# A decode kernel that streams its weights: contiguous MLP weights, a block transpose on VectorE, and a head's output weights on three DMA engines

## The chip, the cores and the metric

The kernel runs on one core of a Trainium2 chip. The metric is the device time of one execution in microseconds; the time before is the median of seven runs. A profile of one execution goes with it. All of the work is memory traffic with small computations on it: four sequences, one new token each.

## What is computed

Cut to what matters (B = 4, D = 512, 32 query heads on 8 key/value heads of 128, F = 1792, bfloat16):

```python
xn = layernorm(x)
# attention over the last W = 1024 cached positions, 4 query heads per cache head
q = xn @ wq;  p = softmax(q k^T * 128 ** -0.5);  s = (p v) @ wo
# MLP
h = gelu(layernorm(xn) @ w1 + b1)
g = silu(h @ w2 + b2)
return x + s * g
```

## The kernel before

All loads of weights and caches are issued by SyncE (SP) onto one queue, in the order in which they are used: wq's first half, K of heads 0 and 1, wq's second half, K of heads 2 to 7, V of head 0, w1, V of head 1, w2, V of heads 2 to 7, and last wo in six transfers. One queue is spread over sixteen DMA engines; each transfer raises a semaphore by 16 when all of it is there. `kv_buf` has eight slots, so V of a head is loaded into the slot of the K that has been transposed (L205 waits for `t_last`). wo's loads (L475) wait for nothing. The small loads of x, b1, b2 and of x in 16 rows (`x16`, L251, in two parts of eight rows) are issued by ScalarE (ACT).

A little planner (`_Program`) keeps one list of operations per engine, in the order in which the code adds them, and puts semaphore waits ahead of an operation. The order on TensorE (PE) is thus that of the code: transposes of K in groups of eight (`T`, L278) run eight groups ahead of the scores (`S`, L297). Then, per head, `PV` (L315) with a product that sums the probabilities (L321); VectorE (DVE) follows with the epilogue (L328 to L333) that divides. Around head 0 to 2 stand the MLP's parts.

The first MLP layer (`mlp1`, L395) has the four tokens, padded to 32 columns, as the stationary operand, and w1 as the moving one. The 14 chunks of 128 hidden values are covered by four column groups of the PE array, `K0 = (0, 4, 8, 10)`, each of 512 columns, with an overlap. Its moving operand is taken in steps: hidden value `p * 14 + k` belongs to chunk k, so that a chunk can be contracted with w2's rows as they lie in memory. GELU runs over 128 by 512 values (L410 to L419). `mlp2` turns the result with four PE transposes (L424) and a copy (L429); `mlp3` multiplies by w2 (L442); `mlp4` makes the gate `g_sb`.

At the end the heads' outputs `OTb` (hidden index on partitions) have to stand as wo's rows do: with `wo_r`, partition p of a head holds the four rows 4p to 4p+3, a contiguous 4 KB. `to_rows` (L486) does that with 16 matmuls by the selector `sel`, and a cast to `OW` (L493). `wo` (L507) then multiplies, transfer by transfer as they land: heads 0 and 1, 2 and 3, 4 and 5, head 6, three of head 7's four rows, and its last row. Each transfer's matmuls have wo as the stationary operand (128 by 128) and four columns moving. L534 multiplies by the gate, L538 turns 16 columns into 16 rows, L540 adds x16, L542 stores.

Of the kernel before, what the change touches and what calls it, by code (L numbers as in the profile page):

```python
# [16 lines left out]
class _Program:  # L17
# [10 lines left out]
    def add(self, eng, fn, *deps):  # L28
        op = _Op(eng, fn, deps)
        self.ops[eng].append(op)  # L30
        return op
# [42 lines left out]
def bass_recurrent_scan__sliding_block_cached__mixer_channel_mlp__decode_kernel(  # L74
# [14 lines left out]
    ALU = mybir.AluOpType  # L89
    AF = mybir.ActivationFunctionType  # L90
    AX = mybir.AxisListType
    BF16 = dt.bfloat16
    F32 = dt.float32

    B, D = 4, 512
    HQ, HKV, DH = 32, 8, 128
# [3 lines left out]
    F = B_w1.shape[1]  # L100
    FC = F // 128
    NC = 32
    KR = W // NC
    UT = 8
# [17 lines left out]
    wo_sb = sb([128, HKV, 4, D], BF16)  # L122
    w1_sb = sb([128, 4, F], BF16)
    w2_sb = sb([128, FC, D], BF16)
    kt_buf = sb([128, NKT, UT * 128], BF16)
    P_buf = sb([128, HKV, NC * 16], BF16)

# [31 lines left out]
    b2_sb = sb([4, 128], BF16)  # L159
    sel = sb([128, 4, 32], BF16)  # L160
    OW = sb([128, 4, HKV * 4], BF16)
    hT = sb([128, 64], BF16)

    OTb = sb([128, HKV * 16], BF16)
    den_sb = sb([128, HKV * 16], F32)
# [38 lines left out]
    def load_v(g):  # L204
        d_v[g] = pg.dma("sp", "v%d" % g, lambda e: e.dma_start(  # L205
            kv_buf[:, (HKV + g) % NS, :, :].rearrange("p c d -> p (c d)"), cache_rows(A_v_cache, g)),
            t_last[(HKV + g) % NS] if HKV + g >= NS else None)
# [11 lines left out]
    for g in range(2, HKV):  # L219
# [11 lines left out]
    c_sel = add("gp", lambda e: e.affine_select(  # L231
        sel[:, :, :], ones_bf[:, :], [[1, 4], [4, 32]], ALU.is_equal, 0.0,
        base=0, channel_multiplier=-1), c_1)
    c_xT = add("gp", lambda e: e.memset(xT[:, :, :], 0.0))
    c_yT = add("gp", lambda e: e.memset(yT[:, :, :], 0.0))
    c_z = add("gp", lambda e: e.memset(zero_bf[:, :], 0.0))
# [4 lines left out]
    c_id32 = add("gp", lambda e: e.affine_select(  # L241
        ident32[:, :], ones32[:, :], [[1, 128]], ALU.is_equal, 0.0,
        base=0, channel_multiplier=-1), c_o32)


    v = add("dve", lambda e: e.tensor_copy(x32[:, :], x_bf[:, :]), d_x)  # L246
# [1 line left out]
    v = add("dve", lambda e: e.bn_aggr(mv1[:, :], st1[:, :]), v)  # L248
    v = add("dve", lambda e: e.tensor_single_scalar(vt1[:, :], mv1[:, 1:2], EPS, ALU.add), v)
    a = add("act", lambda e: e.activation(sq1[:, :], vt1[:, :], AF.Sqrt), v)  # L250
    d_x16 = [pg.dma("act", "x16%d" % i, lambda e, i=i: e.dma_start(  # L251
        x16[8 * i:8 * i + 8, :], x_r[8 * i:8 * i + 8, :])) for i in range(2)]
    v = add("dve", lambda e: e.reciprocal(rstd1[:, :], sq1[:, :]), a)
    v = add("dve", lambda e: e.tensor_scalar(xn32[:, :], x32[:, :], mv1[:, 0:1], rstd1[:, 0:1],
                                             op0=ALU.subtract, op1=ALU.mult), v)
# [10 lines left out]
    cp = {}  # L266
# [116 lines left out]

    K0 = (0, 4, 8, FC - 4)
    mlp = {}

    def f32k(n):

        return kt_buf[:, n, :].bitcast(F32)
    hb = kt_buf[:, 4, 0:512]
    h_ps = psK[0][:, 0:1024].bitcast(F32)

    def mlp1():  # L395
        def fn(pe):
            last = None
            for c in range(4):
                for s in range(4):
                    pe.matmul(psK[0][32 * s:32 * s + 32, 0:1024].bitcast(F32), yT[:, c, :],  # L400
                              bass.AP(w1_sb, c * F + K0[s], [[4 * F, 128], [1, 4], [FC, 128]]),
                              start=(c == 0), stop=False, tile_position=(0, 32 * s))
            for s in range(4):
                last = pe.matmul(psK[0][32 * s:32 * s + 32, 0:1024].bitcast(F32),
                                 ones_bf[0:1, 0:32],
                                 bass.AP(b1_sb, K0[s], [[F, 1], [1, 4], [FC, 128]]),
                                 start=False, stop=True, tile_position=(0, 32 * s))
            return last
        t = add("pe", fn, v_xyT, d_w1, d_b1, *[cp[n] for n in range(NUN - NB, NUN)])
        a = add("act", lambda e: e.activation(f32k(0), h_ps, AF.Square), t)  # L410
        v = add("dve", lambda e: e.scalar_tensor_tensor(f32k(1), f32k(0), 1.0 / GELU_K, h_ps,  # L411
                                                        op0=ALU.add, op1=ALU.mult), a)
        mlp["t"] = add("act", lambda e: e.activation(f32k(2), f32k(1), AF.Tanh,
                                                     scale=GELU_C * GELU_K), v)

    def mlp2():
        v = add("dve", lambda e: e.tensor_scalar(f32k(3), f32k(2), 0.5, 0.5,
                                                 op0=ALU.mult, op1=ALU.add), mlp["t"])
        v = add("dve", lambda e: e.tensor_tensor(hb, f32k(3), h_ps, ALU.mult), v)  # L419

        def fn(pe):
            last = None
            for t in range(4):
                last = pe.transpose(psK[2][:, t * 128:(t + 1) * 128],  # L424
                                    kt_buf[:, 4, t * 128:(t + 1) * 128], ident[:, :])
            return last
        t = add("pe", fn, v, cp[NUN - 1], cp[NUN - 2])

        mlp["h"] = add("dve", lambda e: e.tensor_copy(  # L429
            bass.AP(hT, 0, [[64, 128], [4, 16], [1, 4]]),  # L430
            bass.AP(psK[2], 0, [[1024, 128], [32, 16], [1, 4]])), t)

    def mlp3():
        def fn(pe):
            last = pe.matmul(psM[:, PS_Z:PS_Z + 16], b2_sb[:, :],
                             bass.AP(ident, 0, [[128, 4], [1, 4], [0, 4]]),
                             start=True, stop=False, skip_group_check=True)
            for k in range(FC):
                s = min(k // 4, 2) if k < FC - 4 else 3
                n = (k - K0[s]) * 16 + s * 4  # L440
                for c in range(4):
                    last = pe.matmul(psM[:, PS_Z + c * 4:PS_Z + (c + 1) * 4],  # L442
                                     w2_sb[:, k, c * 128:(c + 1) * 128], hT[:, n:n + 4],
                                     start=False, stop=(k == FC - 1), skip_group_check=True)
            return last
        t = add("pe", fn, mlp["h"], d_w2, d_b2, c_id)
        mlp["tz"] = add("act", lambda e: e.activation(
            tz_sb[:, :], psM[:, PS_Z:PS_Z + 16], AF.Tanh, scale=0.5), t)
# [8 lines left out]
    for n in range(LAG, NUN + LAG):  # L457
# [6 lines left out]
    load_v(1)  # L464
    d_w2 = pg.dma("sp", "w2", lambda e: e.dma_start(
        w2_sb[:, :, :], B_w2.rearrange("(p c) o -> p c o", c=FC)))
    for g in range(2, HKV):
        load_v(g)

    wo_r = A_wo.rearrange("(g p i) o -> p g i o", g=HKV, i=4)  # L470
    d_wo = []
    for n, (g0, g1, i0, i1) in enumerate(((0, 2, 0, 4), (2, 4, 0, 4), (4, 6, 0, 4), (6, 7, 0, 4),
                                          (7, 8, 0, 3), (7, 8, 3, 4))):
        d_wo.append((g0, g1, i0, i1, pg.dma("sp", "wo%d" % n, lambda e, g0=g0, g1=g1, i0=i0, i1=i1:
                                            e.dma_start(wo_sb[:, g0:g1, i0:i1, :],  # L475
                                                        wo_r[:, g0:g1, i0:i1, :]))))

    def to_rows(g0, g1):

        psx = psS[0]  # L480

        def fn(pe):
            last = None
            for i in range(4):
                for j in range(4):
                    last = pe.matmul(psx[32 * j:32 * j + 32, i * 32 + g0 * 4:i * 32 + g1 * 4],  # L486
                                     sel[:, i, :],
                                     bass.AP(OTb, g0 * 16 + j * 4,
                                             [[HKV * 16, 128], [16, g1 - g0], [1, 4]]),
                                     start=True, stop=True)  # L490
            return last
        t = add("pe", fn, ep[g1 - 1], c_sel, ex[HKV - 2])
        return add("dve", lambda e: e.tensor_copy(  # L493
            OW[:, :, g0 * 4:g1 * 4],
            psx[:, 0:128].rearrange("p (i n) -> p i n", i=4)[:, :, g0 * 4:g1 * 4]), t)

    first = [True]

    def wo(k, rows):
        g0, g1, i0, i1, d = d_wo[k]  # L500

        def fn(pe):
            last = None
            for g in range(g0, g1):
                for i in range(i0, i1):
                    for c in range(4):
                        last = pe.matmul(psM[:, PS_W + c * 4:PS_W + (c + 1) * 4],  # L507
                                         wo_sb[:, g, i, c * 128:(c + 1) * 128],
                                         OW[:, i, g * 4:(g + 1) * 4],
                                         start=first[0], stop=(k == len(d_wo) - 1 and i == i1 - 1),  # L510
                                         skip_group_check=True)
                        first[0] = False
            return last
        return add("pe", fn, d, rows, mlp["g"])

    for g in range(HKV):
        PV(g)
        if g == 0:
            epilogue(0)
            mlp1()  # L520
        if g >= 2:
            epilogue(g - 1)
        if g == 1:
            mlp2()
            mlp3()
        if g == 2:
            mlp4()
    epilogue(HKV - 1)
    rows = to_rows(0, HKV)
    for k in range(len(d_wo)):  # L530
        t_w = wo(k, rows)


    v = add("dve", lambda e: e.tensor_tensor(  # L534
# [61 lines left out]
```

## Time and profile before

| | |
|---|---|
| median of 7 runs | 77.05 us (76.97 to 77.1) |
| profiled execution | 77.07 us |
| its span, first to last instruction | 75.3 us |
| mean granted TensorE clock | 0.829 |
| busy: PE, weight loads, DVE, ACT, POOL | 51.3, 39.5, 39.2, 9.8, 4.6 us |
| moved by DMA | 28.99 MB in 4219 packets |
| code fetched on queue q8 | 8 packets, 0.13 MB |
| first MLP layer, L400: 16 matmuls | 4.9 us busy, 1085 ns each |
| query projection, L362: 32 matmuls | 1.9 us busy, 380 ns each |
| output product, L507: 128 matmuls | 3.9 us busy, 166 ns each |

The granted clock of TensorE is at 0.9 or more of full speed in the first 28 of 40 slices of the span and at about half in the last ones. Matmuls overlap, so a group's busy time is shorter than the number of matmuls times the mean of one. A row of the time line gives start, length (both in us), engine, line, operation, target and source, count, and in brackets how long the engine was idle before and what released it. SPq and ACTq are the queues' issuing instructions. In the chain of work that ended last, "issue" is time for which the profile shows no reason.

### The profile page before, as it was taken

The page shows a single profiled execution, that of the slowest core. Times are in us where ns is not written, and L with a number is a line of the kernel's source. Part 1 is how long each engine was busy: PE and PEld are TensorE (multiplying, and loading weights), DVE is VectorE, ACT ScalarE, POOL GpSimd, SP SyncE. Part 2 cuts the span into 40 slices and gives each one's busy share as a digit, 9 for nine tenths or more (in the row PEclk, how much of TensorE's full clock was granted, in tenths as well). Part 3 has the DMA queues.
Part 4 walks back from the last instruction along what each step waited for, and adds up shares of the span by engine and source line. Part 5 has one row for each costly group of instructions (what it writes and reads, how often), then busy time and mean ns, then how long its engine had stood idle before and what let it go on. Part 6 is the DMA issues. An engine that isn't in the chain of part 4 may idle for free.

```text
span 75.3 us, 2309 instructions
## 1 busy us (share of the span) xinstructions
PE 51.3 (68%) x1058; PEld 39.5 (52%) x1058; DVE 39.2 (52%) x82; ACT 9.8 (13%) x16; POOL 4.6 (6%) x14
## 2 busy tenths in 40 slices
PE   0000039984779939987996995999069999918760
PEld 0000039973269929977995880104059586518740
DVE  0778106795158957985995505001664679770010
ACT  0611000000180303111130440003300000000000
POOL 6980000000000000000000000000000000000000
PEclk9999999999999999999999997589555555555555
DMA  2899999998999999999999999999999999999700
GB/s 45 244 418 416 429 440 462 453 418 379 418 440 431 418 422 418 435 414 467 411 408 445 418 428 409 427 422 409 418 435 431 425 401 420 420 418 407 269 19 2
DMA packets 4219, 28.99 MB, mean 385 GB/s; under 512 B 493, under 2 KB 625, under 8 KB 1650
## 3 DMA queue, kind: packets, MB, share of 16 engines
q1 hardware_dynamic: 4160, 28.84, 92.2%
q8 instruction: 8, 0.13, 0.6%
q10 hardware_dynamic: 50, 0.01, 0.1%
q14 instruction: 1, 0.01, 0.0%
HBM read 28.85 MB, written 0.00 MB: 383 GB/s over the span
## 4 chain that ended last, share of the span: by engine, by line
DMA 37%; PE 34%; SPq 16%; issue 5%; DVE 5%
DMA wo_sb<-in_A_wo_dram 24%; PE psK L278 21%; SPq L475 15%; DMA kv_buf<-in_A_k_cache_dram 12%; PE psS L297 6%; DVE kt_buf L284 3%; PE psO L362 3%; PE psS L293 2%; DVE q_sb L368 1%; PE psM L507 1%; PE psK L374 1%; PE psK L346 1%; PE psS L538 1%; SPq L212 1%; SPq L205 0%
## 5 line engine op out<-in xcount | busy, mean ns | idle before, releaser
L278 PE MATMUL psK<-ident,kv_buf 128*128 128x128 bf16 x256 | 20.8, 234 | 12.2 <-DMA kv_buf<-in_A_k_cache_dram 10.7
L284 DVE COPY kt_buf<-psK 128x1024 bf16<-128x1024 bf16 x32 | 21.2, 691 | 9.0 <-PE psK L278 8.9
L278 PEld LDWEIGHTS psK<-ident,kv_buf 128*128 128x128 bf16 x256 | 16.8, 106 | 11.5 <-DMA kv_buf<-in_A_k_cache_dram 10.7
L297 PE MATMUL psS<-qT,kt_buf 128*128 128x16 bf16 x256 | 10.4, 169 | 1.3 <-issue 1.3
L297 PEld LDWEIGHTS psS<-qT,kt_buf 128*128 128x128 bf16 x256 | 9.4, 96 | 3.2 <-issue 2.3
L315 PEld LDWEIGHTS psO<-P_buf,kv_buf 128*128 128x128 bf16 x256 | 7.4, 102 | 3.0 <-issue 3.0
L315 PE MATMUL psO<-P_buf,kv_buf 128*128 128x16 bf16 x256 | 8.0, 173 | 0.2
L328 DVE TENSOR_REDUCE den_sb<-psS 128x16 f32<-128x512 f32 x8 | 5.5, 691 | 4.2 <-PE psS L321 4.0
L305 ACT ACTIVATE P_buf<-psS 128x512 bf16<-128x512 f32 x8 | 4.8, 597 | 17.6 <-PE psS L297 17.6
L400 PE MATMUL psK<-w_sb,yT 128*32 128x512 bf16 x16 | 4.9, 1085 | 0.8 <-issue 0.8
L507 PE MATMUL psM<-OW,wo_sb 128*128 128x4 bf16 x128 | 3.9, 166 | 1.2 <-issue 0.6
L507 PEld LDWEIGHTS psM<-OW,wo_sb 128*128 128x128 bf16 x128 | 3.7, 104 | 1.4 <-issue 1.2
L321 PE MATMUL psS<-P_buf,ones_bf 128*128 128x512 bf16 x8 | 4.3, 534 | 0.0
L411 DVE SCALAR_TENSOR_TENSOR kt_buf<-kt_buf,psK 128x512 f32<-128x512 f32 x1 | 0.7, 686 | 6.1 <-ACT kt_buf L410 6.1
L293 PE MATMUL psS<-negm,ind 128*128 128x512 bf16 x8 | 3.0, 380 | 0.0
L534 DVE TENSOR_TENSOR sg_sb<-psM,g_sb 128x16 f32<-128x16 f32 x1 | 0.2, 185 | 4.7 <-PE psM L507 4.7
L400 PEld LDWEIGHTS psK<-w_sb,yT 128*32 128x32 bf16 x16 | 0.5, 114 | 3.6 <-issue 3.6
L369 ACT ACTIVATE q_sb<-psO 128x512 bf16<-128x512 f32 x1 | 0.6, 597 | 13.3 <-PE psO L362 13.3
L331 DVE RECIPROCAL rden<-den_sb 128x16 f32<-128x16 f32 x8 | 2.0, 253 | 0.3
L362 PE MATMUL psO<-wq_sb,xT 128*32 128x512 bf16 x32 | 1.9, 380 | 0.3 <-DVE xT L351 0.3
L424 PE MATMUL psK<-ident,kt_buf 128*128 128x128 bf16 x4 | 0.6, 308 | 2.1 <-DVE kt_buf L419 2.1
L246 DVE CAST P_buf<-x_bf 4x512 f32<-4x512 bf16 x1 | 0.8, 816 | 2.4 <-DMA x_bf<-in_A_x_dram 2.4
(64 smaller groups left out, 28.8 us busy)
## 6 DMA issues: line engine op xcount, KB each, us to landing
kv_buf<-in_A_k_cache_dram SPq DMA_DIRECT2D x8, 1024.0 KB, 19.9
kv_buf<-in_A_v_cache_dram SPq DMA_DIRECT2D x8, 1024.0 KB, 22.7
wq_sb<-in_A_wq_dram SPq DMA_DIRECT2D x2, 2048.0 KB, 11.4
w_sb<-in_B_w_dram SPq DMA_DIRECT2D x2, 1792.0 KB, 28.1
wo_sb<-in_A_wo_dram SPq DMA_DIRECT2D x3, 1024.0 KB, 24.2
wo_sb<-in_A_wo_dram SPq DMA_DIRECT2D x1, 512.0 KB, 21.5
wo_sb<-in_A_wo_dram SPq DMA_DIRECT2D x1, 384.0 KB, 18.2
wo_sb<-in_A_wo_dram SPq DMA_DIRECT2D x1, 128.0 KB, 18.0
```

The costliest lines, as they stand in the source:

```text
L278: last = pe.transpose(psK[n % NB][:, j * 128:(j + 1) * 128], kv_buf[:, g, u * UT + j, :], ident[:, :])
L284: cp[n] = add("dve", lambda e: e.tensor_copy(kt_buf[:, n % NKT, :], psK[n % NB][:, 0:1024]), t, sc.get(n - NKT))
L293: pe.matmul(psS[g % 2][:, 0:512], ind[:, :], negm[:, :], start=True, stop=False, skip_group_check=True)
L297: last = pe.matmul(psS[g % 2][:, c * 16:(c + 1) * 16], kt_buf[:, n % NKT, j * 128:(j + 1) * 128], qT[:, g * 16:(g + 1) * 16], start=False, ...
L305: ex[g] = add("act", lambda e: e.activation(P_buf[:, g, :], psS[g % 2][:, 0:512], AF.Exp, scale=SCALE), sc[n])
L315: last = pe.matmul(pso[:, 0:16], kv_buf[:, (HKV + g) % NS, c, :], P_buf[:, g, c * 16:(c + 1) * 16], start=(c == 0), stop=(c == NC - 1))
L321: den[g] = add("pe", lambda pe: pe.matmul(psS[g % 2][:, 0:512], ones_bf[:, :], P_buf[:, g, :], start=True, stop=True), ex[HKV - 2 + g % 2] ...
L328: v = add("dve", lambda e: e.tensor_reduce(den_sb[:, cs], bass.AP(psS[g % 2], 0, [[512, 128], [1, 16], [16, NC]]), AX.X, ALU.add), den[g])
L362: last = pe.matmul(psO[m // 4][32 * s:32 * s + 32, 0:512], xT[:, c, :], wq_sb[:, c, m * 512:(m + 1) * 512], start=(c == 0), stop=(c == 3), ...
L400: pe.matmul(psK[0][32 * s:32 * s + 32, 0:1024].bitcast(F32), yT[:, c, :], bass.AP(w1_sb, c * F + K0[s], [[4 * F, 128], [1, 4], [FC, 128]]) ...
L475: e.dma_start(wo_sb[:, g0:g1, i0:i1, :], wo_r[:, g0:g1, i0:i1, :]))))
L507: last = pe.matmul(psM[:, PS_W + c * 4:PS_W + (c + 1) * 4], wo_sb[:, g, i, c * 128:(c + 1) * 128], OW[:, i, g * 4:(g + 1) * 4], start=firs ...
```

## The change

Three edits. First, the four column groups of the first MLP layer each take a contiguous quarter of w1's columns (448), and the bias likewise. GELU then runs over 448 columns; its last multiplication writes its result rearranged (column `a * 14 + k` goes to `k * 32 + a`), and a VectorE transpose in blocks of 32 by 32 gives `hT` in place of the PE transposes and the copy. Second, of head 7's wo, rows 0 to 383 are loaded evenly (`w3`, three rows per partition, in two transfers), while the last 128 rows go into a part of `wq_sb` that is free once the query is computed: 120 of them as five rows on each of 24 partitions in two transfers, 8 rows in a third. These are issued after V of head 4 and wait for the query projection. `to_rows` gets two more selectors, 15 more matmuls and two more casts, and the output product begins with those rows. Third, x16 is loaded in three parts of 7, 5 and 4 rows instead of two of 8.

```diff
+    wox_sb = wq_sb[0:44, 0, 0:6 * D].rearrange("p (j o) -> p j o", j=6)
...
+    c_sel3 = add("gp", lambda e: e.affine_select(
+        sel3[:, :, :, :], ones_w, [[-128, 3], [1, 3], [3, 128]], ALU.is_equal, 0.0,
+        base=0, channel_multiplier=-1), c_1)
+    c_sx = add("gp", lambda e: e.memset(selx[:, :, :], 0.0))
+    for h in range(2):
+        c_sx = add("gp", lambda e, h=h: e.affine_select(
+            selx[:, 0:5, 32 * h:32 * h + 12], ones_bf[:, 0:60], [[1, 5], [5, 3], [15, 4]],
+            ALU.is_equal, 0.0, base=60 * h, channel_multiplier=-1), c_1, c_sx)
+    c_sx5 = add("gp", lambda e: e.affine_select(
+        selx[:, 5, 0:8], ones_bf[:, 0:8], [[1, 8]], ALU.is_equal, 0.0,
+        base=120, channel_multiplier=-1), c_1, c_sx)
...
-    d_x16 = [pg.dma("act", "x16%d" % i, lambda e, i=i: e.dma_start(
-        x16[8 * i:8 * i + 8, :], x_r[8 * i:8 * i + 8, :])) for i in range(2)]
+    d_x16 = [pg.dma("act", "x16%d" % i, lambda e, i=i, n=n: e.dma_start(
+        x16[i:n, :], x_r[i:n, :])) for i, n in ((0, 7), (7, 12), (12, 16))]
...
-                              bass.AP(w1_sb, c * F + K0[s], [[4 * F, 128], [1, 4], [FC, 128]]),
+                              w1_sb[:, c, s * FS:(s + 1) * FS],
...
-                                 bass.AP(b1_sb, K0[s], [[F, 1], [1, 4], [FC, 128]]),
+                                 ones_bf[0:1, 0:32], b1_sb[0:1, s * FS:(s + 1) * FS],
...
-        v = add("dve", lambda e: e.tensor_tensor(hb, f32k(3), h_ps, ALU.mult), v)
-
-        def fn(pe):
-            last = None
-            for t in range(4):
-                last = pe.transpose(psK[2][:, t * 128:(t + 1) * 128],
-                                    kt_buf[:, 4, t * 128:(t + 1) * 128], ident[:, :])
-            return last
-        t = add("pe", fn, v, cp[NUN - 1], cp[NUN - 2])
-
-        mlp["h"] = add("dve", lambda e: e.tensor_copy(
-            bass.AP(hT, 0, [[64, 128], [4, 16], [1, 4]]),
-            bass.AP(psK[2], 0, [[1024, 128], [32, 16], [1, 4]])), t)
+        v = add("dve", lambda e: e.tensor_tensor(
+            bass.AP(kt_buf, 4 * UT * 128, [[NKT * UT * 128, 128], [1, 32], [32, FC]]),
+            f32k(3).rearrange("p (a k) -> p a k", k=FC),
+            h_ps.rearrange("p (a k) -> p a k", k=FC), ALU.mult), v)
+        mlp["h"] = add("dve", lambda e: e.transpose(
+            hT[:, :, :].rearrange("p k n -> p (k n)"), hb), v)
...
     for g in range(HKV):
+        if g >= 2:
+            load_v(g)
+        if g == 4:
+            R3 = (7 * 512 + 384) * D
+            d_wox = [pg.dma("sp", "wox%d" % h, lambda e, h=h: e.dma_start(
+                wox_sb[32 * h:32 * h + 12, 0:5, :].rearrange("p j o -> p (j o)"),
+                bass.AP(A_wo.tensor, R3 + 60 * h * D, [[5 * D, 3], [15 * D, 4], [1, 5 * D]])),
+                t_q) for h in range(2)]
+            d_wox.append(pg.dma("sp", "wox2", lambda e: e.dma_start(
+                wox_sb[0:8, 5, :], bass.AP(A_wo.tensor, R3 + 120 * D, [[D, 8], [1, D]])), t_q))
         PV(g)
...
+    for n, g0 in enumerate((0, 2, 4)):
+        load_wo(n, g0, g0 + 2, 0, 4)
+    load_wo(3, 6, 7, 0, 4)
+
+    w3_r = A_wo[7 * 512:7 * 512 + 384, :].rearrange("(p i) o -> p i o", i=3)
+    d_w3 = [(i0, i1, pg.dma("sp", "w3%d" % i0, lambda e, i0=i0, i1=i1: e.dma_start(
+        wo_sb[:, 7, i0:i1, :], w3_r[:, i0:i1, :]))) for i0, i1 in ((0, 2), (2, 3))]
...
+            for i in range(3):
+                for j in range(3):
+                    last = pe.matmul(psx[:, 128 + i * 4:132 + i * 4], sel3[:, j, i, :],
+                                     OTb[:, o + j * 4:o + j * 4 + 4],
+                                     start=(j == 0), stop=(j == 2))
+            for a in range(6):
+                last = pe.matmul(psx[0:44, 160 + a * 4:164 + a * 4], selx[:, a, :],
+                                 OTb[:, o + 12:o + 16], start=True, stop=True)
...
+    rows = to_rows()
+    wo([(wox_sb[:, a, :], OWx[:, a * 4:(a + 1) * 4], a == 0, False) for a in range(5)]
+       + [(wox_sb[0:8, 5, :], OWx[0:8, 20:24], False, False)], rows[2], mlp["g"], *d_wox)
+    for g0, g1, i0, i1, d in d_wo:
+        wo([(wo_sb[:, g, i, :], OW[:, i, g * 4:(g + 1) * 4], False, False)
+            for g in range(g0, g1) for i in range(i0, i1)], d, rows[0], mlp["g"])
+    for i0, i1, d in d_w3:
+        t_w = wo([(wo_sb[:, 7, i, :], OW3[:, i * 4:(i + 1) * 4], False, i == 2)
+                  for i in range(i0, i1)], d, rows[1])
```

More of the change, by code (lines that the diff above doesn't have):

```diff
@@ L161, in bass_recurrent_scan__sliding_block_cached__mixer_channel_mlp__decode_kernel @@
     OW = sb([128, 4, HKV * 4], BF16)
-    hT = sb([128, 64], BF16)
+    sel3 = sb([128, 3, 3, 128], BF16)
+    selx = sb([128, 6, 44], BF16)
+    OW3 = sb([128, 12], BF16)
+    OWx = sb([44, 24], BF16)
+    hT = sb([128, FC, 32], BF16)
     OTb = sb([128, HKV * 16], BF16)
@@ L243, in bass_recurrent_scan__sliding_block_cached__mixer_channel_mlp__decode_kernel @@
         base=0, channel_multiplier=-1), c_o32)
+    ones_w = bass.AP(ones_bf, 0, [[128, 128], [0, 9], [1, 128]])
+    c_sel3 = add("gp", lambda e: e.affine_select(
[9 more added lines that the diff above has]
+        base=120, channel_multiplier=-1), c_1, c_sx)
     v = add("dve", lambda e: e.tensor_copy(x32[:, :], x_bf[:, :]), d_x)
@@ L382, in bass_recurrent_scan__sliding_block_cached__mixer_channel_mlp__decode_kernel @@
             bass.AP(psK[1], k * 512, [[1024, 128], [32, 4], [1, 4], [128, 4]])), t_qT)
-    K0 = (0, 4, 8, FC - 4)
+    FS = F // 4
     mlp = {}
     def f32k(n):
-        return kt_buf[:, n, :].bitcast(F32)
-    hb = kt_buf[:, 4, 0:512]
-    h_ps = psK[0][:, 0:1024].bitcast(F32)
+        return kt_buf[:, n, 0:2 * FS].bitcast(F32)
+    hb = kt_buf[:, 4, 0:FS]
+    h_ps = psK[0][:, 0:2 * FS].bitcast(F32)
     def mlp1():
@@ L399, in fn @@
                 for s in range(4):
-                    pe.matmul(psK[0][32 * s:32 * s + 32, 0:1024].bitcast(F32), yT[:, c, :],
-                              bass.AP(w1_sb, c * F + K0[s], [[4 * F, 128], [1, 4], [FC, 128]]),
+                    pe.matmul(psK[0][32 * s:32 * s + 32, 0:2 * FS].bitcast(F32), yT[:, c, :],
+                              w1_sb[:, c, s * FS:(s + 1) * FS],
                               start=(c == 0), stop=False, tile_position=(0, 32 * s))
             for s in range(4):
-                last = pe.matmul(psK[0][32 * s:32 * s + 32, 0:1024].bitcast(F32),
-                                 ones_bf[0:1, 0:32],
-                                 bass.AP(b1_sb, K0[s], [[F, 1], [1, 4], [FC, 128]]),
+                last = pe.matmul(psK[0][32 * s:32 * s + 32, 0:2 * FS].bitcast(F32),
+                                 ones_bf[0:1, 0:32], b1_sb[0:1, s * FS:(s + 1) * FS],
                                  start=False, stop=True, tile_position=(0, 32 * s))
@@ L438, in fn @@
             for k in range(FC):
-                s = min(k // 4, 2) if k < FC - 4 else 3
-                n = (k - K0[s]) * 16 + s * 4
                 for c in range(4):
                     last = pe.matmul(psM[:, PS_Z + c * 4:PS_Z + (c + 1) * 4],
-                                     w2_sb[:, k, c * 128:(c + 1) * 128], hT[:, n:n + 4],
+                                     w2_sb[:, k, c * 128:(c + 1) * 128], hT[:, k, 0:4],
                                      start=False, stop=(k == FC - 1), skip_group_check=True)
@@ L466, in bass_recurrent_scan__sliding_block_cached__mixer_channel_mlp__decode_kernel @@
         w2_sb[:, :, :], B_w2.rearrange("(p c) o -> p c o", c=FC)))
[L467 to L514, printed above, removed]
@@ L528, in bass_recurrent_scan__sliding_block_cached__mixer_channel_mlp__decode_kernel, with load_wo @@
     epilogue(HKV - 1)
-    rows = to_rows(0, HKV)
-    for k in range(len(d_wo)):
-        t_w = wo(k, rows)
+    wo_r = A_wo.rearrange("(g p i) o -> p g i o", g=HKV, i=4)
+    d_wo = []
+    def load_wo(n, g0, g1, i0, i1):
+        d_wo.append((g0, g1, i0, i1, pg.dma("sp", "wo%d" % n, lambda e: e.dma_start(
+            wo_sb[:, g0:g1, i0:i1, :], wo_r[:, g0:g1, i0:i1, :]))))
+    for n, g0 in enumerate((0, 2, 4)):
+        load_wo(n, g0, g0 + 2, 0, 4)
+    load_wo(3, 6, 7, 0, 4)
+    w3_r = A_wo[7 * 512:7 * 512 + 384, :].rearrange("(p i) o -> p i o", i=3)
@@ new lines, in bass_recurrent_scan__sliding_block_cached__mixer_channel_mlp__decode_kernel, with to_rows, fn @@
+    d_w3 = [(i0, i1, pg.dma("sp", "w3%d" % i0, lambda e, i0=i0, i1=i1: e.dma_start(
+        wo_sb[:, 7, i0:i1, :], w3_r[:, i0:i1, :]))) for i0, i1 in ((0, 2), (2, 3))]
+    def to_rows():
+        psx = psS[0]
+        def fn(pe):
+            last = None
+            for i in range(4):
+                for j in range(4):
+                    last = pe.matmul(psx[32 * j:32 * j + 32, i * 28:(i + 1) * 28],
+                                     sel[:, i, :],
+                                     bass.AP(OTb, j * 4, [[HKV * 16, 128], [16, 7], [1, 4]]),
+                                     start=True, stop=True)
+            o = 7 * 16
+            for i in range(3):
[6 more added lines that the diff above has]
+                                 OTb[:, o + 12:o + 16], start=True, stop=True)
+            return last
+        t = add("pe", fn, ep[HKV - 1], c_sel, c_sel3, c_sx, c_sx5, ex[HKV - 2])
+        return [add("dve", lambda e: e.tensor_copy(
+            OW[:, :, 0:28], psx[:, 0:112].rearrange("p (i n) -> p i n", i=4)), t),
+            add("dve", lambda e: e.tensor_copy(OW3[:, :], psx[:, 128:140]), t),
+            add("dve", lambda e: e.tensor_copy(OWx[:, :], psx[0:44, 160:184]), t)]
@@ new lines, in wo, with fn @@
+    def wo(tiles, *deps):
+        def fn(pe):
+            last = None
+            for w, o, st, sp in tiles:
+                for c in range(4):
+                    last = pe.matmul(psM[:, PS_W + c * 4:PS_W + (c + 1) * 4],
+                                     w[:, c * 128:(c + 1) * 128], o,
+                                     start=(st and c == 0), stop=sp, skip_group_check=True)
+            return last
+        return add("pe", fn, *deps)
+    rows = to_rows()
+    wo([(wox_sb[:, a, :], OWx[:, a * 4:(a + 1) * 4], a == 0, False) for a in range(5)]
+       + [(wox_sb[0:8, 5, :], OWx[0:8, 20:24], False, False)], rows[2], mlp["g"], *d_wox)
```

## The prediction, made before the result was known

> **What bounds the kernel now.** I read the page's DMA rows first, then the chain that ended last in order of time, then the trace's packets. The page:
>
> ```profile
> DMA  2899999998999999999999999999999999999700
> ...
> q1 hardware_dynamic: 4160, 28.84, 92.2%
> q8 instruction: 8, 0.13, 0.6%
> ```
>
> From slice 3 to 37 the DMA engines are at 0.8 to 0.9 and more: the kernel streams 28.84 MB without a pause, so only the end of that stream can set the time. The chain after the last loads were issued:
>
> ```profile
> 53.67 18.16 DMA wo_sb<-in_A_wo_dram
> 71.84 0.04 issue
> 71.88 0.62 PE psM L507 x16
> 72.50 0.02 issue
> 72.53 0.20 DVE sg_sb L534
> ```
>
> The chain rides the queue from 53.67 to 71.84 us, where the fifth wo transfer lands; then 12 matmuls, then the sixth transfer and its 4 matmuls. The time after the last landing is fixed.
>
> Next, the sixteen completion records of the sixth transfer, one per DMA engine: 70.44, 70.49, 70.52, 70.52, 70.55, 70.63, 70.78, 70.79 | 71.37 | 71.94, 71.95, 72.02, 72.03, 72.03, 72.10, 72.18 us. All engines carry the same bytes, yet eight finish about 1.45 us before seven others. The packet records say why. An 8 KB packet takes 309 ns; each 16 KB packet of queue 8 (instruction code; starts 25.6, 32.1, 38.4, 44.5, 50.5, 60.6, 67.9 and 71.2 us) takes 0.88 to 0.96 us in the first seven, and the data packet behind it is about 0.5 us longer (813 against 309 ns). Seven fetches, seven late engines; an 8 KB fetch on queue 14 at 41.2 us (309 ns) leaves one in between. The stream ends at 72.18 because of the late ones, while the mean of all sixteen is 71.27. That 0.9 us is all that shifting bytes could win.
>
> **The change: the last head's wo.** Before, its 512 KB is 32 KB per engine in two transfers. After, 384 KB goes out evenly (24 KB each, `w3`), 120 rows go in two transfers of 12 partitions by 5 KB and 8 rows in a third, queued behind V of head 4. [...]
>
> Working per engine, by the 8 KB packet's pace (309 ns less the 3 ns overlap: 26.8 B/ns):
> - Thirteen engines: 8 KB less, 0.31 us earlier; five of them get 1 KB of the third transfer, +0.05 (46 ns a packet). The late ones go from 72.18 to 71.87 to 71.92.
> - The lowest three: -0.31, +40 KB in eight packets of 5 KB = 1.53 us, +0.05: +1.27. By the packets' own lengths (5 KB on the line through 4 KB, 159 ns, and 8 KB: 1.55; 2 KB for 3 KB on the line through 46 and 121 ns: -0.30) it is +1.30, with two more semaphore packets +1.31. I take +1.29.
>
> Where do those three stand? Following packets (next start = last end less 3 or 4 ns) the engine with b1's 3584 B packet stays among the eight early ones, likely as their last; for the other two it isn't certain, since engines of nearly equal phase can be confused. The latest of three drawn from the eight early records is 70.71 on average: 70.71 + 1.29 = 72.00, which I take. From the earliest trio (70.52) it is 71.81, and the late engines decide at 71.9; from the last, 70.79, it is 72.08 to 72.12. [...] So the last landing is 72.00 (71.9 to 72.12) in place of 72.18: 0.18 us less.
>
> [...]
>
> **The change: code.** PE gets 35 more matmuls in the tail (to_rows 16 to 31, output 128 to 148) and loses 4 transposes: 31 pairs, 62 instructions. [...] By the trace the eighth fetch, now at 71.2 when nothing is left to delay, comes some 60 instructions earlier in the program, near 68 to 70 us, and makes one more engine late: nothing if that is an unloaded early one (70.7 - 0.3 + 1.4 = 71.8), but 73.4 if it is one of the loaded three. I take nothing, and keep the other end as a rival.
>
> **The change: first MLP layer.**
>
> ```profile
> 44.94 1.07 PE L400 MATMUL psK<-w_sb,yT 128*32 128x512 bf16 x1
> 46.84 3.82 PE L400 MATMUL psK<-w_sb,yT 128*32 128x512 bf16 x15 [0.83 <-issue]
> ...
> 50.58 1.07 PE L404 MATMUL psK<-b_sb,ones_bf 1*32 1x512 bf16 x4
> 51.59 0.87 PEld L315 LDWEIGHTS psO<-P_buf,kv_buf 128*128 128x128 bf16 x32 [0.91 <-issue]
> ```
>
> Five groups of four matmuls take 0.9 to 1.0 us each where the moving operand jumps 28 bytes. The contiguous counterpart is L362: 32 matmuls in 1.94 us, 0.24 us for four. Four groups after the pause at 46.84 (a code fetch) then end near 47.8 instead of 51.6: 3.8 us of PE time. 448 columns for 512 may save a little more. The multiplication that now writes in strides replaces 0.69 us (L419); nearest rows 0.61 to 0.69, doubled if strides hurt: +0.7 at most. The block transpose has no row; four PE transposes and a copy took 0.61 + 0.19 us plus waits. [...] So mlp3 begins near 51.5 instead of 55.8. None of it shortens the path: PV of head 7 can't start before its V lands at 62.16. It is cover for the tail. There PE now does:
>
> ```profile
> 67.14 0.30 PE L486 MATMUL psS<-OTb,sel 128*32 128x32 bf16 x16 [1.30 <-DVE OTb L333]
> 67.51 0.29 DVE L493 CAST OW<-psS 128x128 bf16<-128x128 f32 x1 [0.42 <-PE psS L486]
> ...
> 67.95 1.55 PE L507 MATMUL psM<-OW,wo_sb 128*128 128x4 bf16 x53 [0.51 <-DVE OW L493]
> 70.09 2.40 PE L507 MATMUL psM<-OW,wo_sb 128*128 128x4 bf16 x75 [0.58 <-issue]
> ```
>
> After: PV 7 from 62.2, its denominator and epilogue as before 2.7 us later at 65.0, rows 0.5, three casts 0.7 behind them, so the wox matmuls start at 66.2 (24 at 26.7 ns: 0.65) and heads 0 and 1 (0.86) end at 67.7, before the second transfer at 67.22 is used up at 68.6. Then PE waits for each landing with about 1 us in hand (before it had 0.2). Without the MLP part the added 15 + 24 matmuls less 4 and two casts, some 1.3 us, would have made PE late: that is the cover's price. Behind the new wait for wox stands the whole output product, but wox, queued ahead of V 5, lands before 60 us.
>
> The tail keeps its form: the last transfer (1 KB rows) is followed by 4 matmuls. POOL builds three more selectors (about 1430 elements, at L237's 1852 ns for 512 some 5 us) after all others and by 10 us; they are needed at 65. SP issues three more loads of 0.5 us with a queue of 10 us ahead of it; ACT one more x16 load, early: no charge.
>
> **Sum.** The profiled execution took 77.07 with a span of 75.3 (1.77 outside); the median is 77.05. 77.05 - 0.18 = 76.87.
>
> **Rivals.**
> 1. *As above*, 0.70: last landing 71.9 to 72.12, 76.77 to 76.99. Faster 0.50, within 0.2% (0.15 us, about what a measurement of this kernel can tell) 0.20.
> 2. *A code fetch on a loaded engine* (slower), 0.22. The three lowest are only as good as their lead of 1.4 us. The in-between engine at 71.37 + 1.29 = 72.66: +0.5, 77.5. A full fetch, 72.0 + 1.4 = 73.4: +1.2, 78.3. It decides as soon as any engine of the three gets a fetch costing over 0.3 us. For: seven of sixteen engines are hit, the eighth fetch moves forward. [...]
> 3. *PE becomes the bound* (slower), 0.08: fetch pauses (0.75 us at 69.34 now) fall in the longer tail and eat the 1 us in hand. Half a microsecond over: 77.5.
> That the change doesn't do what it says (sixteen engines used after all) gives 77.05, and lies in the 0.20.
>
> **What would show it.** The last transfer's completions within 0.4 us for late and loaded engines; idle PE before the last w3 matmuls; L400's counterpart near 0.25 us a group; the eighth q8 packet before 71 us. Wrong: a lone completion beyond 72.3, or PE busy up to its last output matmul without a DMA wait. Range: 76.72 (late engines decide and x16 helps) to 77.6 (the first price of rivals 2 and 3).

## The result and the profile after

| | before | after |
|---|---|---|
| median | 77.06 us (33 runs; 77.05 in the first 7) | 76.84 us (14 runs, 76.71 to 77.02) |
| ratio to before | | 0.9971, 95% interval 0.9962 to 0.9979 |
| profiled execution | 77.07 us, span 75.3 | 76.93 us, span 75.2 |
| packets, code packets of queue 8 | 4219, 8 | 4265, 8 |

The change takes 0.22 us off. A ratio, here and below, leaves out runs that took over 1.5% longer than the fastest of the same kernel; none of these did. The page after shows the same filled stream as before; the first digits of the DMA row and the two queues:

```profile
DMA  1999999999999999999999999999999999999800
...
q1 hardware_dynamic: 4206, 28.84, 92.4%
q8 instruction: 8, 0.13, 0.6%
```

Nothing has been taken out of it: the bytes of q1 are the same, with 46 packets more. The chain that ended last, after (start, length, what):

```profile
51.54 19.63 DMA wo_sb<-in_A_wo_dram
71.18 0.05 issue
71.22 0.59 PE psM L555 x16
71.81 0.04 issue
71.85 0.61 PE psM L555 x12
72.46 0.02 issue
72.48 0.20 DVE sg_sb L572
```

It rides the DMA queue as before, then PE from the landing of head 6 (71.18) on: 28 matmuls in three groups (16, 8 and 4), of which the last 4 belong to the transfer that lands last. The gate's multiplication comes 0.35 us after the last landing, exactly as before (72.53 less 72.18, 72.48 less 72.13). So the end is again the last landing. The completion records of the last transfer, one per DMA engine, from the traces:

```
before      70.44 70.49 70.52 70.52 70.55 70.63 70.78 70.79 | 71.37 | 71.94 71.95 72.02 72.03 72.03 72.10 72.18
after       70.24 70.27 70.49 70.50 70.53 | 71.47 | 71.59 71.73 71.76 71.77 71.79 71.81 71.86 71.92 71.95 72.13
```

Eight early engines have become five, seven late ones ten: three engines were moved over on purpose. The seven had a mean of 72.04, the ten have one of 71.83. The packets of wox can be counted: 24 of 5120 B, in three chains with 193 ns from start to start, 1.55 us on each chain. The records carry no engine's number, but the very last, 72.13, can be followed back by its distance from the others: two of the three loaded engines landed the second wox transfer at 54.84 and 54.88, the third at 55.05, and from V of head 5 (57.53) on one record comes 0.13 to 0.22 us behind all others in every transfer. I read it as that third engine. This pair of profiles shows only 0.05 us at the last landing; the two profiled executions lie 0.14 apart (the other 0.09 us lie behind the landing), and the medians 0.22. Executions of one kernel scatter by 0.1 to 0.2 us, so I read the mechanism from several traces below and the size from the medians.

The PE side of the change, from the time line after:

```profile
47.09 1.68 PE L421 MATMUL psK<-w_sb,yT 128*32 128x448 bf16 x15 [1.81 <-issue]
...
51.59 2.08 DVE L440 TENSOR_TENSOR kt_buf<-kt_buf,psK 128x448 bf16<-128x448 f32 x1
53.70 0.65 DVE L444 STREAM_TRANSPOSE hT<-kt_buf 128x448 bf16<-128x448 bf16 x1
...
54.40 0.19 PE L449 MATMUL psM<-ident,b_sb 4*128 4x16 bf16 x1 [3.75 <-DVE hT L444]
```

A group of four matmuls on contiguous columns starts 0.35 to 0.37 us after the one before (47.09, 47.44, 47.81) where the stepped ones took 0.9. The strided write costs 2.08 us and the second layer starts at 54.4, 1.4 us earlier than before.

### The profile page after: what moved, and what is told of

It is laid out like the page before. It is cut to its first block, busy times and chain, and to the rows that moved or that the text cites. A ratio compares the mean times of both kernels' runs of the same rounds, so it can differ in the third digit from the quotient of the medians.

```text
span 75.2 us, 2384 instructions
## 1 busy us (share of the span) xinstructions
PE 49.4 (66%) x1089; PEld 40.9 (54%) x1089; DVE 41.0 (55%) x84; ACT 9.7 (13%) x16; POOL 7.3 (10%) x19
## 2 busy tenths in 40 slices
DMA packets 4265, 28.99 MB, mean 386 GB/s; under 512 B 507, under 2 KB 647, under 8 KB 1696
## 4 chain that ended last, share of the span: by engine, by line
DMA 39%; PE 36%; SPq 13%; issue 5%; DVE 4%
DMA wo_sb<-in_A_wo_dram 26%; PE psK L299 22%; DMA kv_buf<-in_A_k_cache_dram 13%; SPq L510 12%; PE psS L318 6%; PE psO L383 3%; DVE kt_buf L305 2%; PE psS L314 2%; PE psM L555 2%; DVE q_sb L389 1%; PE psK L395 1%; PE psK L367 1%; PE psS L576 1%; SPq L218 1%; SPq L211 0%
## 5 line engine op out<-in xcount | busy, mean ns | idle before, releaser
L421 PE MATMUL psK<-w_sb,yT 128*32 128x448 bf16 x16 | 2.0, 561 | 1.8 <-issue 1.8
L431 DVE SCALAR_TENSOR_TENSOR kt_buf<-kt_buf,psK 128x448 f32<-128x448 f32 x1 | 0.6, 621 | 3.7 <-ACT kt_buf L430 3.7
L440 DVE TENSOR_TENSOR kt_buf<-kt_buf,psK 128x448 bf16<-128x448 f32 x1 | 2.1, 2082 | 0.0
```

The costliest lines, as they stand in the source:

```text
L440: v = add("dve", lambda e: e.tensor_tensor(bass.AP(kt_buf, 4 * UT * 128, [[NKT * UT * 128, 128], [1, 32], [32, FC]]), f32k(3).rearrange("p ...
```

## Experiments

The theory: the time is the last completion on the DMA engines plus a fixed rest; each code fetch of PE makes one engine 1.4 us late; the change fills three engines that had no fetch with bytes taken from all others. Rivals: the shorter MLP on PE brings the gain; or the order in which small loads fall does.

**The MLP part alone** (before, with contiguous quarters of w1 and the block transpose):

```diff
-    bass.AP(w1_sb, c * F + K0[s], [[4 * F, 128], [1, 4], [FC, 128]]),
+    w1_sb[:, c, s * FS:(s + 1) * FS],
```

> The kernel before with the MLP part of the change alone (contiguous quarters of w1, block transpose); wo and x16 as before. Theory: the gain comes from where the bytes of wo go, and the MLP part only gives PE time. Then the last wo transfer lands at 72.2 us as before and the time is 77.0 to 77.1. Rival: the shorter MLP on PE brings the gain; then 76.85. PE should finish the heads' output product up to the fifth transfer earlier than before (before: 71.63 us), so that it waits for DMA longer.

Measured 76.94 us against 76.94 of before on the same chip, ratio 0.9999 (0.9989 to 1.0008). The last transfer lands at 72.14. Its tail:

```profile
69.72 1.01 PE L498 MATMUL psM<-OW,wo_sb 128*128 128x4 bf16 x32 [1.47 <-DMA wo_sb<-in_A_wo_dram]
70.97 0.58 PE L498 MATMUL psM<-OW,wo_sb 128*128 128x4 bf16 x16 [0.23 <-DMA wo_sb<-in_A_wo_dram]
71.86 0.59 PE L498 MATMUL psM<-OW,wo_sb 128*128 128x4 bf16 x16 [0.31 <-DMA wo_sb<-in_A_wo_dram]
```

Every group waits for DMA, the first for 1.47 us: PE time was gained and is waited away. The first rival falls.

**The wo part alone** (the changed kernel with the first layer, its turn and x16 as before):

```diff
-    w1_sb[:, c, s * FS:(s + 1) * FS],
+    bass.AP(w1_sb, c * F + K0[s], [[4 * F, 128], [1, 4], [FC, 128]]),
```

> The wo part alone (three lowest engines, more selectors and matmuls), MLP and x16 as before. Theory: the landings are those of the changed kernel (last 72.05 to 72.15), but without the 1.4 us that PE gained, PE becomes late: the rows start at 67.1, the first output matmul near 68.6, 148 matmuls at 26.7 ns are 3.95 us and a code fetch pause of some 0.3 to 0.7 us comes in: last matmul near 72.9 to 73.2, time 77.4 to 77.9. Rival: PE keeps up and this part alone gives 76.85.

Measured 76.82 against 76.94, ratio 0.9978 (0.9967 to 0.9989): most or all of the gain, and my price for the missing cover did not come. This kernel has x16 in two parts of eight rows, as before, so the third edit isn't what brings the gain either. Last completions: 70.14 to 70.38 (five), 71.24, then 71.50 to 71.89 (ten). Why PE is not late:

```profile
62.22 1.02 PE L336 MATMUL psO<-P_buf,kv_buf 128*128 128x16 bf16 x32 [0.63 <-DMA kv_buf<-in_A_v_cache_dram]
...
67.28 1.87 PE L564 MATMUL psM<-OW,wo_sb 128*128 128x4 bf16 x64
69.70 1.01 PE L564 MATMUL psM<-OW,wo_sb 128*128 128x4 bf16 x32 [0.55 <-DMA wo_sb<-in_A_wo_dram]
70.92 1.27 PE L564 MATMUL psM<-OW,wo_sb 128*128 128x4 bf16 x28 [0.21 <-DMA wo_sb<-in_A_wo_dram]
```

PV of head 7 starts at 62.22, as soon as its V is there, though this kernel has the long first layer; in the profiled execution of before it started at 64.41. PE's place differs by some 2 us between these two profiles: in that of before it stood still for 1.27, 0.81 and 0.69 us behind the first three code fetches (25.6, 32.1, 38.4 us), while this one asked for its code at 22.1, 29.1 and 35.5 us and ran from 30 to 42 us without a pause. One of its 12 runs, left out of the ratio, took 77.81 us; a late PE or a code fetch on a loaded engine would do that, but it has no profile. Whether the difference belongs to the execution or to the kernel isn't shown (the three profiles with 40 matmuls more, below, ask first at 24.7 to 25.2 us); what sets how early PE asks stays open.

**b1 in sixteen pieces, x16 in one transfer**:

```diff
-        b1_sb[0:1, :], B_b1.rearrange("(o n) -> o n", o=1)))
+        b1_sb[0:1, :, 0:F // 16], B_b1.rearrange("(o a n) -> o a n", o=1, a=16)))
...
-        x16[i:n, :], x_r[i:n, :])) for i, n in ((0, 7), (7, 12), (12, 16))]
+    d_x16 = [pg.dma("act", "x16", lambda e: e.dma_start(x16[:, :], x_r[:, :]))]
```

> The changed kernel with b1 loaded in 16 pieces of 224 B (one per DMA engine) instead of 3584 B on one engine, and x16 in one transfer of 16 rows. Theory: in the changed kernel the last landing (72.13) is that of the lowest engine, which carries b1 (140 ns) and three packets of x16 beside the 40 KB; without them it ends 0.14 to 0.15 us earlier, and the code-fetch engines (71.95, +0.03 to +0.05 by the spread packets) are level with it: last landing 71.98 to 72.02, time 0.10 to 0.15 us under the changed kernel's 76.84, 76.70 to 76.75. Rival: the last landing is a code-fetch engine's; then nothing changes or it gets 0.05 us longer, 76.84 to 76.9.

Measured 76.73 against 76.94, ratio 0.9970 (0.9959 to 0.9981), the changed kernel's own ratio. The profile agrees with the step (late and loaded engines end within 71.56 to 71.78), but traces of kernels without this edit end at 71.85 to 71.91 too, two with 40 matmuls more at 71.99 and 72.03, and both edits together (below) at 71.92: a gain of some 0.1 us, which isn't resolved. That b1 and three packets of x16 lie on one of the loaded engines is not shown, since the records carry no engine's number.

**Dense write of the last GELU product**:

```diff
-            bass.AP(kt_buf, 4 * UT * 128, [[NKT * UT * 128, 128], [1, 32], [32, FC]]),
-            f32k(3).rearrange("p (a k) -> p a k", k=FC),
-            h_ps.rearrange("p (a k) -> p a k", k=FC), ALU.mult), v)
+            bass.AP(kt_buf, 4 * UT * 128, [[NKT * UT * 128, 128], [32, FC], [1, 32]]),
+            f32k(3).rearrange("p (a k) -> p k a", k=FC),
+            h_ps.rearrange("p (a k) -> p k a", k=FC), ALU.mult), v)
```

> The changed kernel; the last GELU multiplication runs in the order in which it writes (its output dense, its two inputs in steps of 14 elements) instead of writing every element 64 bytes from the one before. In the changed kernel it took 2.08 us. Theory: the write stride is what costs; dense it takes 0.6 to 0.8 us, the MLP's second layer starts 1.3 us earlier, and since all of it lies beside the DMA stream the time stays that of the changed kernel (ratio to before 0.997). Rival: the strided inputs cost as much (2 us); the time is then the same too, which is why the row is looked at.

```profile
49.56 0.91 DVE L440 TENSOR_TENSOR kt_buf<-kt_buf,psK 128x448 bf16<-128x448 f32 x1
50.51 0.65 DVE L444 STREAM_TRANSPOSE hT<-kt_buf 128x448 bf16<-128x448 bf16 x1
```

0.91 us for 2.08, above the 0.6 to 0.8 that I expected: the stepped inputs cost some (all dense, 512 columns took 0.69 us in L419 of before), the stepped write 1.17 more. Time 76.67 against 77.00, ratio 0.9964 (0.9952 to 0.9977, five runs), not told apart from the changed kernel. **Both edits together**, the version meant to be best:

> The changed kernel with b1 on sixteen engines, x16 in one transfer and the dense multiplication together. Theory: as with b1 and x16 alone, which gave a ratio of 0.9970 to before at a last landing of 71.78; the dense write adds PE slack and no time. 0.996 to 0.9975. Rival: PE slack matters in some executions (code fetch pauses), then it gets better than either, 0.995.

76.78 against 77.00, ratio 0.9974 (0.9964 to 0.9984). Neither adds anything that the runs resolve; the kernel of the change was not beaten.

**Four engines instead of three** (32 rows on each of four):

```diff
-                wox_sb[32 * h:32 * h + 12, 0:5, :].rearrange("p j o -> p (j o)"),
-                bass.AP(A_wo.tensor, R3 + 60 * h * D, [[5 * D, 3], [15 * D, 4], [1, 5 * D]])),
+                wox_sb[32 * h:32 * h + 16, 0:4, :].rearrange("p j o -> p (j o)"),
+                bass.AP(A_wo.tensor, R3 + 64 * h * D, [[4 * D, 4], [16 * D, 4], [1, 4 * D]])),
```

> The changed kernel with the last 128 rows of wo on the four lowest engines (two transfers of 16 partitions with four rows each, 32 KB an engine) instead of 120 rows on three and 8 rows on eight. Theory of the fetches: each loaded engine gets 1.24 us more and 0.31 less, so it stays under a late one if it has no fetch: 70.8 + 0.95 = 71.75. If the fourth engine is an early one, the last landing is a late engine's, 71.9, and the time is 0.1 us under the changed kernel's or equal (ratio 0.996 to 0.997). If it is the one in between (71.2 before the load), it ends at 72.4: 0.3 us over the changed kernel, ratio 1.000 to 1.002. If it is one with a full fetch, 73.1: ratio 1.010 to 1.013.

Measured 77.28 against 77.00, ratio 1.0045 (1.0031 to 1.0059): slower than before. The first wox transfer lands at 53.75, 53.84, 53.90 and, on one engine, 55.04; the last two of the sixteen records of the last wo transfer stand at 71.90 and 72.69:

```profile
71.79 1.22 PE L550 MATMUL psM<-OW,wo_sb 128*128 128x4 bf16 x28 [0.27 <-DMA wo_sb<-in_A_wo_dram]
73.04 0.18 DVE L567 TENSOR_TENSOR sg_sb<-psM,g_sb 128x16 f32<-128x16 f32 x1 [5.88 <-PE psM L550]
```

PE waits for that one engine, and the last landing is 0.5 us behind that of before. The fourth engine is already 1.2 us late when wox arrives. Four packets of 4 KB take 0.62 us (159 ns each in before and after, less 3 ns of overlap), so it stood at 54.42 before them; that is the first of the six late records of V of head 4, where I place the engine in between. That one stands at 71.47 in the trace after, and 71.47 + 1.24 = 72.71 agrees with 72.69. By these sums it is the middle one of the three cases expected, a little dearer than its 72.4. By the same sums four fails here not by the size of the load but because the fourth engine had been held up by a code fetch: the prediction's second rival at the lower of its two prices, 77.5 (77.50 in the profiled run, 77.28 in the median). That it is the fourth by number is not shown.

**More code in front of the tail** (40 unused matmuls where PE waits for the MLP's turn):

```diff
+        def spare(pe):
+            for i in range(40):
+                last = pe.matmul(psM[:, 300:304], ident[:, :], ident[:, 0:4], start=True, stop=True,
+                                 skip_group_check=True)
+            return last
+        add("pe", spare, c_id)
```

> The changed kernel with 40 unused matmuls (80 PE instructions, into an unused part of PSUM) put where PE waits for the MLP's transpose. They cost no time there. They move each later code fetch 80 instructions forward: the eighth from 69.97 us to some 68.5 to 69. Theory: a fetch makes the DMA engine it falls on 1.4 us late; the eighth one falls on an engine that had just finished in the changed kernel (70.24), which now ends at 71.7, still below 72.1: time unchanged, 76.8 to 76.9, with ten engines late by a fetch or by load in the changed kernel and eleven here. Rival 2 of the prediction: it falls on one of the three loaded engines: last landing 73.5, time 78.2.

The profiled run (76.70) did as expected: eighth fetch at 69.06, four early engines left, last landing 71.91. But of 12 runs seven took 76.70 to 77.04 and five 77.38 to 77.50 (ratio 1.0016, 0.9992 to 1.0040). Half of the extra code, 20 matmuls:

> The changed kernel with 20 unused matmuls (40 PE instructions) where the run with 40 had two groups of times, 76.7 to 77.0 and 77.4 to 77.5. In the profiled one of those a ninth code fetch starts at 72.5, after the output product. Theory a: the slow group waits for the code of that ninth block at the end of PE's program; with 20 matmuls there is no ninth block, and all times lie within 76.65 to 77.0. Theory b: the slow group has a fetch on an engine that is still loading; with the eighth fetch near 69.5 it can happen here too, times up to 77.5 remain.

All 11 runs within 76.63 to 76.89, ratio 0.9972 (0.9963 to 0.9982): 40 instructions more cost nothing. With 60:

> The changed kernel with 60 unused matmuls (120 PE instructions) in the same place. Theory a (the slow times of the run with 40 wait for a ninth code block that PE needs at the end of its program): with 40 instructions more, the ninth block is needed earlier in the program and by every execution; its fetch starts before 72.4 or all times lie in or near the slow group, 77.3 to 77.8, without a completion of the last wo transfer beyond 72.2. Theory b (a fetch on a loaded engine): the times follow the last completion, 72.5 or more in a slow one.

76.71 to 78.27, ratio 1.0006 (0.9989 to 1.0024) over the ten runs that the ratio keeps, median of all twelve 77.16. The two that it leaves out, 78.00 and 78.27, have no profile; a fetch on a loaded engine, priced at 78.2, isn't excluded for them. This time the profiled execution was one of the long ones, 77.51:

```profile
67.78 2.68 PE L561 MATMUL psM<-OW,wo_sb 128*128 128x4 bf16 x85
71.75 1.18 PE L561 MATMUL psM<-OW,wo_sb 128*128 128x4 bf16 x39 [1.29 <-issue]
72.97 0.18 DVE L578 TENSOR_TENSOR sg_sb<-psM,g_sb 128x16 f32<-128x16 f32 x1 [6.06 <-PE psM L561]
```

The last wo transfer has landed at 71.86, as it should. PE stands still for 1.29 us in the middle of a transfer's matmuls, with nothing in the profile that it waits for, and goes on at 71.75 with 39 matmuls left. The eighth code fetch had started at 69.44, 2.31 us before. Two more executions of the kernel with 40:

> The run with 40 unused matmuls again, for a profile of a slow execution, if it falls on one. Theory a: in one of 77.4 the last wo transfer lands near 71.9 as in the fast one and the time is lost after it, in a pause of PE or of the engines' last meeting behind the ninth fetch. Theory b: the last completion is late by the 0.6 us that the slow times show.

> As the run before: a second try for a profile of a slow execution of the kernel with 40 unused matmuls. Theory a: time lost after the last landing, behind the ninth fetch. Theory b: last landing 0.6 us later.

76.99 and 76.83 us. The first:

```profile
71.11 0.40 PE L561 MATMUL psM<-OW,wo_sb 128*128 128x4 bf16 x9 [0.22 <-DMA wo_sb<-in_A_wo_dram]
71.85 0.65 PE L561 MATMUL psM<-OW,wo_sb 128*128 128x4 bf16 x19 [0.35 <-issue]
```

PE stops after nine matmuls and resumes at 71.85; the eighth fetch started at 69.51, 2.34 us before. In the second it resumes at 71.70 after a fetch at 69.37: 2.33 us. In the long execution that was caught (60 matmuls) both theories a and b fall: its ninth fetch starts at 72.86 and its last landing is on time. What costs there, as I read it, is that PE needs the code of the eighth fetch before the last landing, and goes on only some 2.3 us after that fetch began. The execution of before has the same pause: fetch 67.86, PE's last matmul ahead of it begins at 69.34, the next at 70.09, 2.23 us after the fetch. I read these pauses as waits for code, by the fetch ahead of each and by the count of PE's records ahead of it: 449, 705, 961, 1217 and 1985, in before and after alike, so all lie whole multiples of 256 records apart. With 40 or 60 matmuls more the pause in the tail comes after 2229 records in all three traces, 1020 behind the one at 1209, within four records of four times 256. No profile caught one of 77.4 with 40 matmuls; that it is this pause, a little longer, is argued from the three that were caught.

## Why the prediction was right, step by step

*The end is the last landing plus a fixed rest*: held. In every profile here in which PE kept up, time less last landing is the same (before 77.07 - 72.18 = 4.89; the others 4.79 to 4.82):

| profiled | last landing | time |
|---|---|---|
| before | 72.18 | 77.07 |
| MLP part alone | 72.14 | 76.94 |
| after | 72.13 | 76.93 |
| wo part alone | 71.89 | 76.69 |
| 20 matmuls more | 71.86 | 76.66 |
| b1 and x16 spread | 71.78 | 76.60 |
| four engines | 72.69 | 77.50 |
| 60 matmuls more (PE late) | 71.86 | 77.51 |
| 40 matmuls more, second profile (PE late) | 71.99 | 76.99 |

Before and the MLP part alone end at 72.18 and 72.14; the ten traces with three loaded engines end at 71.78 to 72.13, with a mean of 71.92. That is 0.24 us less, and the medians say 0.22.

*Loaded engines to 72.00, late ones to 71.87 to 71.92, 0.18 us less*: the trace after has 72.13 and 71.95, and the measured gain is 0.22. The 72.13 is the case that the prediction named, the engine with b1 as the last of the early ones, "72.08 to 72.12". That it is the engine with b1 isn't shown; that it was the last of the early ones is, as far as records can be followed. The loaded engines' own term held: 1.55 us for the eight packets of 5 KB. No run sends the same 128 rows through the same code over all sixteen engines, so that the choice of engines makes the gain rests on these records and on the run with four. The mechanism was right; the size agrees within the scatter of executions and isn't better known than that.

*Three engines, the lowest by number, with 40 KB each, and five others with 1 KB*: no run shows which engines a transfer takes, because the records carry no number. What the trace after shows in its place is how many: three chains for the two transfers of 12 partitions, eight packets of 1 KB for the third, and seven, five and four data completions for the three parts of x16. Nor does a run show the help from x16 that the low end of the range, 76.72, counts on: with x16 in two parts (the wo part alone) the median was 76.82, with three (the change) 76.84.

*The packets' pace, 26.8 B/ns, and 1.53 us for the 40 KB*: held, 1.55 us for both transfers on each engine, and landings of the two 0.80 to 0.83 us apart. In the filled queue packets of 5 KB follow each other at 26.5 B/ns, as those of 8 KB do at 26.8.

*The eighth fetch, near 68 to 70 us, at no cost*: it came at 69.97 and cost nothing, but "makes one more engine late" did not show there: five engines stayed early, as many as the three moved ones leave. In the ten traces with three loaded engines five stay early when it starts at 69.81 to 70.12, and four when it starts at 69.06 to 69.51 (40 or 60 matmuls more); none of the last landings is beyond 72.13.

*The first layer near 47.8 and mlp3 near 51.5*: mis-sized. The layer's end was 49.2 and mlp3 began at 54.4. A group of four took 0.37 us, not 0.24: the granted clock fell from 1.0 to 0.5 at 46.55 us, and the one matmul ahead of the fall took 363 ns, those behind it 554 to 581; L362 had run at 1.0. (In before the clock stands at 0.9 or more in the first 24 slices only, not 28: it is 0.5 from 46.04 to 49.45 us, then 1.0 until 52.87. The stepped matmuls took 1069 to 1094 ns at either clock.) PE also stood still for 1.81 us behind a code fetch in the layer; the write in steps cost 2.08 us where the doubled row gave at most 1.4; and the 0.5 us for the block transpose in the 51.5 was my estimate, which no run shows: the transpose took 0.65. Hidden, as predicted, so nothing of it reaches the sum.

*"Without the MLP part the added 15 + 24 matmuls less 4 and two casts, some 1.3 us, would have made PE late"*: wrong: in the profile of the wo part alone PE waits for DMA up to the end, and eleven of its twelve runs lie at 76.64 to 76.97. I read PE's place in the tail from one profile in which code pauses had put it 2 us back. *PE about 1 us in hand*: mis-sized too. After, PV of head 7 began at 62.98, not 62.2, the wox matmuls at 67.21, not 66.2, and the group before head 6 ended 0.13 us before its landing:

```profile
68.81 2.24 PE L555 MATMUL psM<-OW,wo_sb 128*128 128x4 bf16 x79 [0.18 <-issue]
71.22 1.22 PE L555 MATMUL psM<-OW,wo_sb 128*128 128x4 bf16 x28 [0.17 <-DMA wo_sb<-in_A_wo_dram]
```

In most other traces with three loaded engines PE waited 0.5 to 0.6 us for heads 4 and 5 and 0.2 to 0.3 for head 6.

*Rivals 2 and 3*: neither shows in the changed kernel's 14 runs, both exist. An engine with a fetch under the load puts the time 0.28 us over the median of before (four engines). Runs of 77.4 and more appear with 80 more PE instructions and did not with 40; in the one that was profiled, with 120, it is a code pause in the tail. The changed kernel stands that near to both.

## What to carry over

When a kernel is bound by a filled DMA queue, look at when each engine finishes the last transfer, not at the mean rate: here eight of sixteen were idle for the last 1.4 us, and moving 40 KB to each of three of them paid 0.3%. Count the code of the busiest engine as DMA traffic: here a fetch held one DMA engine back by some 1.4 us (the early and the late records of before lie 1.45 us apart in the mean), and PE, where it had to wait for the code, went on some 2.3 us after the fetch began. Before an edit that "makes room" on an engine is credited, try it alone: here it gave nothing (ratio 0.9999).

## What the runs showed of the hardware that was not expected

- A 16 KB code packet in the filled stream takes 0.88 to 0.97 us (the last one, at the stream's end, up to 1.29), the 8 KB data packet behind it about 0.5 us longer than usual (a 4 KB one 0.28); pauses of PE behind a fetch end 2.15 to 2.50 us after it starts. None of the three loaded engines was hit before 54 us in any of the ten traces with three (their first wox landings lie at 53.77 to 54.25 us), nor was one of them late at the end; the fourth engine was, in the one trace that could show it.
- A VectorE product of 128 by 448 that writes bfloat16 every 64 bytes took 2.08 us, with dense writes and inputs in steps of 14 elements 0.91 us. The 32 by 32 block transpose of 128 by 448 took 0.65 us.
- PE's place in the tail differed by 2.2 us between two profiles with the same long first layer (PV of head 7 at 62.22 us in the wo part alone, 64.41 in before), while their last landings lay 0.3 us apart.
